# A reordered head: where four tiles of a layer norm get their scale, and which engine empties their transposes

## The chip, the cores and the metric

The kernel runs on one core of a Trainium2 chip. The metric is the device time of one execution in microseconds (us). The engines of the core are named as the profile names them: PE is TensorE, PEld its weight loads, DVE is VectorE, ACT is ScalarE, POOL is GpSimd, and SP is SyncE, which here only issues DMAs. Each engine works through its own queue in order; engines wait for each other through semaphores.

## The reference

One input x of 2048 rows by 512 columns is layer-normalized, and two branches read the normalized rows: a diagonal state-space model (branch A) and a gated feed-forward network (branch B). The output is the sum of x and both branches.

```python
xn = _layernorm(x, axis=-1)                      # (x - mean) / sqrt(var + 1e-5)
# A: complex state of 512, h[t] = Lam_bar * h[t-1] + B_bar xn[t]
#    y[t] = 2 Re(C h[t]) + xn[t] * Dskip
# B: (silu(xn @ w_gate) * (xn @ w_up)) @ w_down,  w_gate and w_up 512 x 1376
return x + A(xn) + B(xn)
```

Input and output are bf16.

## The kernel before

The 2048 rows are 16 tiles of 128 rows (`NT`), four tiles to a chunk (`TPC`), four chunks (`NCH`). TensorE needs the normalized rows transposed, with the 512 columns on the partitions, in `xnT`: four column blocks (`KD`), of which the first two and the last two are here called the first and the second contraction half (`HK` is two). Everything behind the head runs chunk by chunk: gate and up projections (`gu_mm`, L421), input projections of the state-space model (`bproj_tile`, L346), rotations and scans on VectorE (L356 to L388), and two output products (L501, L510). VectorE's work there is put into a list with a cost for each item, and `pump` issues items as TensorE's work is issued. The kernel is written under a manual schedule: each engine does its instructions in the order of the program text.

The head, L596 to L650, takes the first chunk's four tiles one by one, while their loads come in, so that TensorE can start before the chunk is complete. For a tile n it needs:

- statistics (`bn_stats`, `bn_aggr` on VectorE) that give mean and variance in `mv`;
- `rstd`, the reciprocal root. There are two ways: `rstd_act` (L177) takes a logarithm and an exponential on ScalarE, both within the table set loaded at L596; `ln_rstd` (L182) adds epsilon on VectorE and takes a power on POOL (L184);
- `norm_dve` (L190), the normalization on VectorE, here in place in `xall`;
- `xT_pe` (L202): four transposes by TensorE, two into each of two PSUM tiles, and for each PSUM tile a copy into `xnT`, by ScalarE (L218) or VectorE (L216). With `prm_too` a small transpose of twelve parameter rows (L239) is written behind the second pair.

Then `head_mm(which, lo, hi, ks, fis)` (L588) issues, for the gate (`which` 0) or the up weights (1), the matmuls of tiles lo to hi, over the column blocks `ks`, for the weight column blocks `fis`. The results of the first three weight blocks (`H`) accumulate in six PSUM banks that are held until all four tiles are through. `dummy(n, cols)` issues n matmuls on ones into one of these banks, before it is used.

The order of the text before: all rstd but tile 0's come from POOL. ScalarE copies the transposes of tiles 0, 1 and 2, VectorE those of tile 3. Tile 1 is normalized in two halves of 256 columns; tile 2's statistics are taken in two halves around them (L606, L609). TensorE takes tile 0's gate matmuls first, both contraction halves, and puts tile 1's transposes between its up matmuls. Tile 3's transposes stand in the midst of tile 2's up matmuls. An `iota` for a later table is issued on POOL at L623.

After the head's matmuls `params_a`, `params_a2` and `params_sin` compute small parameters (with a table load on ScalarE at L248), and L650 on is the steady part. The first matmul behind the head is the first of line L421. The transposes of later chunks are made by DMA (L223).

Of the kernel before, what the change touches and what calls it, by code (L numbers as in the profile page):

```python
# [10 lines left out]
F32 = mybir.dt.float32  # L11
# [12 lines left out]
def kernel(  # L24
# [17 lines left out]
    nc = tc.nc  # L42
    _, L, D = A_x.shape
# [3 lines left out]
    CW = 512  # L47
# [4 lines left out]
    KD = D // 128  # L52
# [11 lines left out]
    const = ctx.enter_context(tc.tile_pool(name="const", bufs=1))  # L64
# [8 lines left out]
    def bank(shape=(128, CW), dtype=F32):  # L73
        return psum.tile(list(shape), dtype, name="ps")
# [10 lines left out]
    xall = const.tile([128, NT, D], BF16, name="xall")  # L85
# [4 lines left out]
    for gi, (a, b) in enumerate(fgroups):  # L90
        cols = min(F, b * 128) - a * 128
# [12 lines left out]
    def wslice(groups, fi, k):  # L104
        for (a, b), t in zip(fgroups, groups):
            if a <= fi < b:
                return t[:, k, (fi - a) * 128:(fi - a) * 128 + fsz[fi]]
# [48 lines left out]
    ident = const.tile([128, 128], BF16, name="ident")  # L156
    make_identity(nc, ident[:])
    jidx = const.tile([128, CW], F32, name="jidx")


    stats = const.tile([128, NT, 6], F32, name="stats")
    stats2 = const.tile([128, 2, 6], F32, name="stats2")
    mv = const.tile([128, NT, 2], F32, name="mv")
    ve = const.tile([128, NT], F32, name="ve")
    rstd = const.tile([128, NT], F32, name="rstd")
# [4 lines left out]
    def xn_tile(c):  # L170
        return xn_end if c == NCH - 1 else xall[:, c * TPC:(c + 1) * TPC, :]

    def ln_stats(n):
        nc.vector.bn_stats(out=stats[:, n, :], in_=xall[:, n, :])  # L174
        nc.vector.bn_aggr(out=mv[:, n, :], in_=stats[:, n, :])  # L175

    def rstd_act(n):  # L177

        nc.scalar.activation(out=ve[:, n:n + 1], in_=mv[:, n, 1:2], func=ACT.Ln, bias=eps_t[:, 0:1])
        nc.scalar.activation(out=rstd[:, n:n + 1], in_=ve[:, n:n + 1], func=ACT.Exp, scale=-0.5)  # L180

    def ln_rstd(a, b):  # L182
        nc.vector.tensor_scalar(out=ve[:, a:b], in0=mv[:, a:b, 1], scalar1=EPS, scalar2=None, op0=ALU.add)  # L183
        nc.gpsimd.tensor_tensor(out=rstd[:, a:b], in0=ve[:, a:b], in1=neg_half[:, 0:b - a], op=ALU.pow)  # L184
# [2 lines left out]
        nc.vector.scalar_tensor_tensor(out=nb[:, a:b], in0=mv[:, a:b, 0], scalar=-1.0, in1=rstd[:, a:b],  # L187
                                       op0=ALU.mult, op1=ALU.mult)

    def norm_dve(n, cols=slice(0, D)):  # L190
        c, i = divmod(n, TPC)
        nc.vector.tensor_scalar(out=xn_tile(c)[:, i, cols], in0=xall[:, n, cols], scalar1=mv[:, n, 0:1],  # L192
                                scalar2=rstd[:, n:n + 1], op0=ALU.subtract, op1=ALU.mult)

    def norm_act(n):
# [3 lines left out]

    HK = KD // 2  # L200

    def xT_pe(n, halves=(0, 1), on_dve=False, prm_too=False):  # L202

        c, i = divmod(n, TPC)
        for h in halves:
            tp = bank((128, HK * 128 + 3 * NQ), BF16)
            for k in range(HK):
                lo = (h * HK + k) * 128
                nc.tensor.transpose(out=tp[:, k * 128:(k + 1) * 128], in_=xn_tile(c)[:, i, lo:lo + 128],  # L209
                                    identity=ident[:])  # L210
            if prm_too and h == 1:
                prm_transpose(tp[:, HK * 128:])
            dst = xnT[:, h * HK:(h + 1) * HK, n * 128:(n + 1) * 128]
            src = tp[:, 0:HK * 128].rearrange("p (k t) -> p k t", k=HK)
            if on_dve:
                nc.vector.tensor_copy(out=dst, in_=src)  # L216
            else:
                nc.scalar.copy(out=dst, in_=src)  # L218
        return tp[:, HK * 128:]
# [18 lines left out]
    def prm_transpose(pp):  # L238
        nc.tensor.transpose(out=pp, in_=prm_rows[:], identity=ident[0:3 * NQ, 0:3 * NQ])  # L239
# [5 lines left out]
    def params_a2():  # L245
        V.tensor_tensor(out=dre[:], in0=dt_t[:], in1=lre, op=ALU.mult)
        nc.scalar.activation(out=r_t[:], in_=dre[:], func=ACT.Exp)
        nc.scalar.preload_act_table_set("silu_and_others")  # L248
        V.scalar_tensor_tensor(out=ws2[:, 0, :], in0=dt_t[:], scalar=INV_2PI, in1=lim, op0=ALU.mult, op1=ALU.mult)
# [37 lines left out]
    def params_sin():  # L287

        def turns(dst, shift):
            src = ws2[:]  # L290
            if shift:
                V.tensor_scalar(out=dst[:], in0=src, scalar1=shift, scalar2=None, op0=ALU.add)
                src = dst[:]
            V.tensor_scalar(out=kk[:], in0=src, scalar1=MAGIC, scalar2=MAGIC, op0=ALU.add, op1=ALU.subtract)
            tt(dst[:], src, kk[:], ALU.subtract)

        V.tensor_scalar(out=ws2[:, 1, :], in0=ws2[:, 0, :], scalar1=float(CW), scalar2=None, op0=ALU.mult)
        turns(fs1, 0.0)
        nc.scalar.activation(out=sin1[:], in_=fs1[:], func=ACT.Sin, scale=TWO_PI_LO)
        turns(fc1, 0.25)  # L300
        nc.scalar.activation(out=cos1[:], in_=fc1[:], func=ACT.Sin, scale=TWO_PI_LO)
# [261 lines left out]
    H = 3  # L563
# [3 lines left out]
    def dummy(n, cols):  # L567
        for _ in range(n):
            nc.tensor.matmul(warm[:, 0:cols], lhsT=ones[:, 0:128], rhs=ones[:, 0:cols], start=True, stop=True)  # L569

    def ln_rest(c, on_act):
        ops = [(0.7, lambda n=n: ln_stats(n)) for n in range(c * TPC, (c + 1) * TPC)]
        def fin():
            ln_rstd(c * TPC, (c + 1) * TPC)
        def nbf():
            ln_nb(c * TPC, (c + 1) * TPC)
        ops += [(0.1, fin)]
        tail = [(0.1, nbf)] if on_act else []
        for n in range(c * TPC, (c + 1) * TPC):
            def one(n=n):  # L580
                (norm_act if on_act else norm_dve)(n)
                xT_dma(n)
            tail.append((0.05 if on_act else 0.35, one))
        return ops, tail
# [3 lines left out]
    def head_mm(which, lo, hi, ks, fis):  # L588

        for fi in fis:  # L590
            for k in ks:
                nc.tensor.matmul(held[fi][which][:, lo * 128:hi * 128], lhsT=wslice((wg_g, wu_g)[which], fi, k),  # L592
                                 rhs=xnT[:, k, lo * 128:hi * 128], start=(k == 0), stop=(k == KD - 1))

    allk = range(KD)
# [3 lines left out]
    rstd_act(0)  # L599
    nc.vector.bn_stats(out=stats[:, 1, :], in_=xall[:, 1, :])  # L600
    norm_dve(0)
    nc.vector.bn_aggr(out=mv[:, 1, :], in_=stats[:, 1, :])
    ln_rstd(1, 2)
    xT_pe(0)
    dummy(6, 128)
    nc.vector.bn_stats(out=stats2[:, 0, :], in_=xall[:, 2, 0:D // 2])  # L606
    norm_dve(1, slice(0, D // 2))
    norm_dve(1, slice(D // 2, D))
    nc.vector.bn_stats(out=stats2[:, 1, :], in_=xall[:, 2, D // 2:D])  # L609
    nc.vector.bn_aggr(out=mv[:, 2, :], in_=stats2[:].rearrange("p h s -> p (h s)"))  # L610
    ln_rstd(2, 3)

    head_mm(0, 0, 1, range(0, HK), (0, 1))
    head_mm(0, 0, 1, range(HK, KD), (0, 1))
    xT_pe(1, (0,))
    head_mm(1, 0, 1, allk, (0,))
    xT_pe(1, (1,))
    head_mm(1, 0, 1, allk, (1,))
    nc.vector.bn_stats(out=stats[:, 3, :], in_=xall[:, 3, :])
    norm_dve(2)  # L620
    nc.vector.bn_aggr(out=mv[:, 3, :], in_=stats[:, 3, :])
    ln_rstd(3, 4)
    nc.gpsimd.iota(out=jidx[:], pattern=[[1, CW]], base=0, channel_multiplier=0,  # L623
                   allow_small_or_imprecise_dtypes=True)
    head_mm(0, 1, 2, range(0, HK), (0, 1))
    head_mm(0, 1, 2, range(HK, KD), (0, 1))
    head_mm(1, 1, 2, allk, (0, 1))
    head_mm(0, 0, 2, allk, (2,))
    pp = xT_pe(2, prm_too=True)
    head_mm(1, 0, 2, allk, (2,))  # L630
    norm_dve(3)
    params_a(pp)
    params_a2()
    head_mm(0, 2, 3, range(0, HK), range(H))
    head_mm(0, 2, 3, range(HK, KD), range(H))
    head_mm(1, 2, 3, allk, (0,))
    xT_pe(3, on_dve=True)
    head_mm(1, 2, 3, allk, (1, 2))
    params_sin()
    tables = table_ops()  # L640
    stats1, norm1 = ln_rest(1, False)
# [60 lines left out]
    stats2, norm2 = ln_rest(2, True)  # L702
# [68 lines left out]
```

## Time and profile before

| | |
|---|---|
| time, median of 3 runs | 180.82 us (180.65 to 181.29) |
| profiled execution, its time | 180.69 us |
| its span in the profile | 178.9 us |
| PE busy | 173.6 us (97%) |
| DVE busy | 153.4 us (86%) |
| ACT busy | 93.8 us (52%) |
| POOL busy | 24.9 us (14%) |
| DMA | 15.53 MB, mean 87 GB/s |
| first transpose of tile 0 (L209) starts | 5.64 us |
| first matmul of L421 starts | 12.99 us |

The span is what the profile sees, from the first to the last instruction; the time of the execution has 1.79 us more around it. A row of the timeline gives the start, the time from the first start to the last end, the engine, the line, the operation, what is written and read, and the count; in brackets stands the idle time of the engine in front of it and what ended it. Matmuls are pipelined: one row's duration is longer than the distance between two starts.

### The profile page before, as it was taken

How to read it: one execution, taken by the hardware profiler on the slowest of the kernel's cores; microseconds unless marked ns; L12 is line 12 of the kernel's file. 1: busy time of each engine (PE TensorE's matmuls, PEld its weight loads, DVE VectorE, ACT ScalarE, POOL GpSimd, SP SyncE). 2: the span in 40 equal slices, each digit the busy share in tenths (PEclk: the TensorE clock that was granted, in tenths of full speed). 3: DMA queues.
4: the chain of work that ended last, by engine and by line, in shares of the span. 5: the costliest groups of instructions: out<-in, count | busy, mean ns of one | idle time of the engine just before them, and what ended most of it. 6: DMA issues, size and time to landing. Idle time of an engine off the chain costs nothing.

```text
span 178.9 us, 2451 instructions
## 1 busy us (share of the span) xinstructions
PE 173.6 (97%) x904; PEld 83.5 (47%) x920; DVE 153.4 (86%) x234; ACT 93.8 (52%) x170; POOL 24.9 (14%) x32
## 2 busy tenths in 40 slices
PE   8899999999999999999999999999999999999993
PEld 3684444443444444444444444444444444444743
DVE  1879997999999999999999999999999999950033
ACT  2469876988399957022998661014866610230000
POOL 5223000000500000027200000013405000150000
DMA  6999557994138400021930000007295900073012
GB/s 158 316 288 217 104 107 198 346 182 93 26 64 234 179 0 0 0 20 15 132 72 2 0 0 4 0 0 67 33 135 73 166 2 0 0 79 38 4 47 70
DMA packets 29515, 15.53 MB, mean 87 GB/s; under 512 B 18336, under 2 KB 29440, under 8 KB 29472
## 3 DMA queue, kind: packets, MB, share of 16 engines
q1 hardware_dynamic: 24416, 11.21, 26.4%
q0 software_dynamic: 3456, 3.28, 14.4%
q10 hardware_dynamic: 1632, 0.89, 1.7%
q8 instruction: 7, 0.11, 0.3%
q14 instruction: 4, 0.03, 0.1%
HBM read 8.03 MB, written 5.24 MB: 74 GB/s over the span
## 4 chain that ended last, share of the span: by engine, by line
PE 95%; DMA 2%; DVE 1%; issue 1%
PE ps L421 36%; PE ps L501 21%; PE ps L346 15%; PE ps L510 15%; PE ps L592 3%; PE ps L447 2%; DMA xall<-in_A_x_dram 2%; PE ps L457 1%; PE ps L209 1%; DVE stats L174 0%; DVE stats L600 0%; DVE xall L192 0%; PE ps L569 0%; DVE res L513 0%; DVE mv L175 0%
## 5 line engine op out<-in xcount | busy, mean ns | idle before, releaser
L501 PE MATMUL ps<-wd_sb,guT 128*128 128x512 bf16 (+4 forms) x195 | 38.6, 355 | 0.2
L421 PE MATMUL ps<-xnT,wg 128*128 128x512 bf16 x143 | 37.6, 379 | 0.3
L421 PE MATMUL ps<-xnT,wu 128*128 128x512 bf16 x146 | 37.6, 379 | 0.1
L388 DVE TENSOR_TENSOR_SCAN g<-r_t,car,u 128x512 bf16<-128x512 f32 x24 | 28.9, 1262 | 0.0
L510 PE MATMUL ps<-CF,wt 128*128 128x512 bf16 (+2 forms) x140 | 28.1, 355 | 0.2
L346 PE MATMUL ps<-xnT,BT 128*128 128x512 bf16 x126 | 28.2, 379 | 0.1
L501 PEld LDWEIGHTS <-guT 128*128 128x128 bf16 (+1 forms) x198 | 18.5, 98 | 19.9
L516 ACT CAST res<-ps 128x512 bf16<-128x512 f32 x12 | 7.0, 585 | 38.3 <-PE ps L510 38.3
L435 ACT ACTIVATE guT<-ps 128x512 bf16<-128x512 f32 x40 | 24.8, 619 | 3.6 <-PE ps L421 3.4
L436 ACT CAST u<-ps 128x512 bf16<-128x512 f32 x40 | 24.2, 606 | 4.0 <-PE ps L421 4.0
L517 POOL DMA_DIRECT2D out_dram<-res x12 | 11.1, 999 | 86.9 <-ACT res L516 86.9
L421 PEld LDWEIGHTS <-wu 128*128 128x128 bf16 x148 | 14.5, 98 | 17.5
L421 PEld LDWEIGHTS <-wg 128*128 128x128 bf16 x148 | 14.3, 98 | 17.6 <-issue 0.8
L510 PEld LDWEIGHTS <-wt 128*128 128x128 bf16 x144 | 13.4, 98 | 14.3
L346 PEld LDWEIGHTS <-BT 128*128 128x128 bf16 x128 | 12.5, 98 | 15.1
L348 ACT CAST u<-ps 128x512 bf16<-128x512 f32 x32 | 17.5, 590 | 2.9 <-PE ps L346 2.8
L513 DVE TENSOR_TENSOR res<-ps,xn_end 128x512 bf16<-128x512 f32 (+2 forms) x6 | 3.0, 514 | 14.4 <-PE ps L510 14.4
L440 DVE TENSOR_TENSOR guT<-guT,u 128x1024 bf16<-128x1024 bf16 x20 | 13.5, 680 | 0.0
L184 POOL TENSOR_TENSOR rstd<-ve,neg_half 128x1 f32<-128x1 f32 (+1 forms) x6 | 6.9, 1155 | 40.2 <-DVE ve L183 40.2
L174 DVE BATCH_NORM_STATS2 stats<-xall 128x6 f32<-128x512 bf16 x13 | 8.7, 669 | 2.8 <-DMA xall<-in_A_x_dram 2.8
L356 DVE TENSOR_TENSOR pm<-u,c 128x2048 bf16<-128x2048 bf16 x8 | 9.8, 1220 | 1.2 <-ACT c L273 1.1
L356 DVE TENSOR_TENSOR pm<-g,c 128x2048 bf16<-128x2048 bf16 x8 | 9.7, 1217 | 0.1
(105 smaller groups left out, 158.2 us busy)
## 6 DMA issues: line engine op xcount, KB each, us to landing
out_dram<-in_A_x_dram SPq DMA_DIRECT2D x1, 1536.0 KB, 7.9
out_dram<-res POOLq DMA_DIRECT2D x12, 128.0 KB, 3.1
out_dram<-xall POOLq DMA_DIRECT2D x3, 512.0 KB, 5.9
wd_sb<-in_B_w_down_dram SPq DMA_DIRECT2D x1, 1280.0 KB, 10.1
xall<-in_A_x_dram SPq DMA_DIRECT2D x1, 1024.0 KB, 6.4
wg<-in_B_w_gate_dram SPq DMA_DIRECT2D x2, 384.0 KB, 5.4
wu<-in_B_w_up_dram SPq DMA_DIRECT2D x2, 384.0 KB, 5.6
wu<-in_B_w_up_dram ACTq DMA_DIRECT2D x2, 256.0 KB, 5.2
```

Source lines behind the costliest of these rows:

```text
L174: nc.vector.bn_stats(out=stats[:, n, :], in_=xall[:, n, :])
L346: nc.tensor.matmul(ps[:], lhsT=BT[:, part, k, q * 128:(q + 1) * 128], rhs=xnT[:, k, c * CW:(c + 1) * CW], start=(k == 0), stop=(k == KD - 1))
L348: nc.scalar.copy(out=u_tiles[c][:, part, q, :], in_=ps[:])
L356: V.tensor_tensor(out=t[:], in0=flat(src()[:, i]), in1=flat(tab[:]), op=ALU.mult)
L388: V.tensor_tensor_scan(out=g()[:, part, q, :], data0=r_t[:, q:q + 1].to_broadcast([128, CW]), data1=u_tiles[c][:, part, q, :], initial=ini ...
L421: nc.tensor.matmul(ps[:fs, lo:hi], lhsT=wslice(groups, fi, k), rhs=xnT[:, k, c * CW + lo:c * CW + hi], start=(k == 0), stop=(k == KD - 1))
L435: nc.scalar.activation(out=guT[:fs, fi, :], in_=psg[:fs], func=ACT.Silu)
L436: nc.scalar.copy(out=u_pair[c][:fs, fi % 2, :], in_=psu[:fs])
L440: products.append(lambda: V.tensor_tensor(out=g, in0=g, in1=u, op=ALU.mult))
L501: nc.tensor.matmul(o[:], lhsT=gu_tiles[c][:fsz[fi], fi, i * 128:(i + 1) * 128], rhs=wd_sb[:fsz[fi], fi, lo:hi], start=(fi == 0), stop=False)
L510: nc.tensor.matmul(o[:], lhsT=w_tiles[c][:, part, q, i * 128:(i + 1) * 128], rhs=CF[:, part, q, lo:hi], start=False, stop=(part == 1 and q ...
L517: nc.gpsimd.dma_start(out=out_v[:, n, lo:hi], in_=res[:, lo:hi], accum_op=ALU.add)
```

## The change

All edits lie in the head and in the two helpers that it calls. rstd of tiles 1, 2 and 3 comes from ScalarE like tile 0's. Their places in ScalarE's queue are: tile 1's before the copy of tile 0, tile 2's behind the copies of tile 1, and tile 3's behind tile 2's. `xT_pe` takes the set of halves that VectorE copies: the first half of tile 0, and both halves of tiles 2 and 3; tile 1 and the second half of tile 0 stay with ScalarE. Tile 1 is normalized whole and tile 2's statistics are taken whole; the tile `stats2` goes. For tiles 0, 1 and 2 TensorE now takes the first contraction half for gate and up and then the second half for both; the transposes of the next tile (1) or of tile 3 stand between the halves. There are four small dummies in place of six, and the iota is issued on POOL right behind the identity.

```diff
@@ constants
     jidx = const.tile([128, CW], F32, name="jidx")
+    nc.gpsimd.iota(out=jidx[:], pattern=[[1, CW]], base=0, channel_multiplier=0, allow_small_or_imprecise_dtypes=True)
-    stats2 = const.tile([128, 2, 6], F32, name="stats2")
@@ helpers
-    def norm_dve(n, cols=slice(0, D)):
+    def norm_dve(n):
...
-    def xT_pe(n, halves=(0, 1), on_dve=False, prm_too=False):
+    def xT_pe(n, on_dve=(), prm_too=False):
...
-        for h in halves:
+        for h in range(2):
...
-            if on_dve:
+            if h in on_dve:
@@ head
-    ln_rstd(1, 2)
-    xT_pe(0)
-    dummy(6, 128)
-    nc.vector.bn_stats(out=stats2[:, 0, :], in_=xall[:, 2, 0:D // 2])
-    norm_dve(1, slice(0, D // 2))
-    norm_dve(1, slice(D // 2, D))
-    nc.vector.bn_stats(out=stats2[:, 1, :], in_=xall[:, 2, D // 2:D])
-    nc.vector.bn_aggr(out=mv[:, 2, :], in_=stats2[:].rearrange("p h s -> p (h s)"))
-    ln_rstd(2, 3)
+    rstd_act(1)
+    xT_pe(0, on_dve=(0,))
+    dummy(4, 128)
+    norm_dve(1)
+    ln_stats(2)
 
     head_mm(0, 0, 1, range(0, HK), (0, 1))
+    head_mm(1, 0, 1, range(0, HK), (0, 1))
+    xT_pe(1)
+    rstd_act(2)
     head_mm(0, 0, 1, range(HK, KD), (0, 1))
-    xT_pe(1, (0,))
-    head_mm(1, 0, 1, allk, (0,))
-    xT_pe(1, (1,))
-    head_mm(1, 0, 1, allk, (1,))
+    head_mm(1, 0, 1, range(HK, KD), (0, 1))
     nc.vector.bn_stats(out=stats[:, 3, :], in_=xall[:, 3, :])
     norm_dve(2)
     nc.vector.bn_aggr(out=mv[:, 3, :], in_=stats[:, 3, :])
-    ln_rstd(3, 4)
-    nc.gpsimd.iota(out=jidx[:], pattern=[[1, CW]], base=0, channel_multiplier=0,
-                   allow_small_or_imprecise_dtypes=True)
+    rstd_act(3)
     head_mm(0, 1, 2, range(0, HK), (0, 1))
+    head_mm(1, 1, 2, range(0, HK), (0, 1))
     head_mm(0, 1, 2, range(HK, KD), (0, 1))
-    head_mm(1, 1, 2, allk, (0, 1))
+    head_mm(1, 1, 2, range(HK, KD), (0, 1))
     head_mm(0, 0, 2, allk, (2,))
-    pp = xT_pe(2, prm_too=True)
+    pp = xT_pe(2, on_dve=(0, 1), prm_too=True)
     head_mm(1, 0, 2, allk, (2,))
     norm_dve(3)
     params_a(pp)
     params_a2()
     head_mm(0, 2, 3, range(0, HK), range(H))
+    head_mm(1, 2, 3, range(0, HK), range(H))
+    xT_pe(3, on_dve=(0, 1))
     head_mm(0, 2, 3, range(HK, KD), range(H))
-    head_mm(1, 2, 3, allk, (0,))
-    xT_pe(3, on_dve=True)
-    head_mm(1, 2, 3, allk, (1, 2))
+    head_mm(1, 2, 3, range(HK, KD), range(H))
```

## The prediction

> **What bounds the kernel now.** I read the page's busy shares and slices first, then the chain that ended last in order of time, then the timeline of the first 14 us engine by engine. The page and the chain:
>
> ```profile
> PE 173.6 (97%) x904; PEld 83.5 (47%) x920; DVE 153.4 (86%) x234; ACT 93.8 (52%) x170; POOL 24.9 (14%) x32
> ...
> PE 95%; DMA 2%; DVE 1%; issue 1%
> ...
> 7.58 1.73 PE ps L592 x24
> 9.31 0.22 PE ps L209 x4
> ...
> 13.43 6.64 PE ps L421 x30
> 20.06 4.10 PE ps L346 x19
> ```
>
> From 12.99 us (the first L421 matmul) to 176 us the chain is TensorE alone, and its matmuls there start every 0.216 us without a hole, apart from single missing records: 30 matmuls of L421 take 6.64 us, 19 of L346 take 4.10. Nothing ahead of 12.99 is hidden by anything, and nothing behind it waits. So the change is worth what it moves the first L421 matmul, one for one, provided that nothing behind it becomes late.
>
> The head, TensorE's timeline and then the three others':
>
> ```profile
> 5.64 0.40 PE L209 MATMUL ps<-ident,xall 128*128 128x128 bf16 x4 [0.81 <-DVE xall L192]
> 5.88 0.51 PE L569 MATMUL ps<-const-bfloat16-1.0 128*128 128x128 bf16 x6
> 6.39 0.66 PE L592 MATMUL ps<-xnT,wg 128*128 128x128 bf16 x8
> 6.96 0.28 PE L209 MATMUL ps<-ident,xall 128*128 128x128 bf16 x2
> ...
> 7.71 0.72 PE L592 MATMUL ps<-xnT,wg 128*128 128x128 bf16 x8
> 8.27 0.61 PE L592 MATMUL ps<-xnT,wu 128*128 128x128 bf16 x8
> ...
> 10.02 0.83 PE L592 MATMUL ps<-xnT,wg 128*128 128x128 bf16 x12
> ```
>
> ```profile
> 4.61 0.29 ACT L179 ACTIVATE ve<-mv,eps_t 128x1 f32<-128x1 f32 x1 [0.55 <-DVE mv L175]
> 4.94 0.20 ACT L180 ACTIVATE rstd<-ve 128x1 f32<-128x1 f32 x1
> 5.97 0.65 ACT L218 COPY xnT<-ps 128x256 bf16<-128x256 bf16 x2 [0.83 <-PE ps L209]
> ```
>
> ```profile
> 5.17 0.41 DVE L192 TENSOR_SCALAR xall<-xall,mv,rstd 128x512 bf16<-128x512 bf16 x1
> ...
> 9.97 0.63 DVE L192 TENSOR_SCALAR xall<-xall,mv,rstd 128x512 bf16<-128x512 bf16 x1 [0.66 <-POOL rstd L184]
> ...
> 11.23 0.49 DVE L216 COPY xnT<-ps 128x256 bf16<-128x256 bf16 x2
> ```
>
> ```profile
> 5.95 0.58 POOL L184 TENSOR_TENSOR rstd<-ve,neg_half 128x1 f32<-128x1 f32 x1 [2.34 <-DVE ve L183]
> ...
> 9.89 0.56 POOL L623 IOTA jidx<- 128x512 f32 x1
> ```
>
> Of a matmul row 0.22 us is its own length; starts lie 0.0555 apart (x12 in 0.83: (0.83-0.22)/11). I call that a slot; a 256-wide matmul is two. From 5.64 to 12.99 are 7.35 us. In it stand 16 transposes, 6 dummies and 88 matmuls, 8 of them wide: 118 slots, 6.55 us, and 0.11 for the parameter transpose. The other 0.69 us are holes, found by adding slots to each start (0.71 by the rounded starts): 0.17 before 6.39 (tile 0's first copy), 0.13 before 6.96 (second copy 0.05, tile 1's normalization 0.08), 0.07 before 7.71 and 0.12 inside the eight that follow (tile 1's two copies), 0.15 around the parameter transpose at 9.47, 0.07 at 11.77 (tile 3's second copy). Those 0.69 and two dummies (0.11) are all that the head can give: 0.80 us.
>
> **The change part by part.** The sum is made against the profiled execution, 180.69 us (span 178.9, 1.79 around it). The median of the three runs, 180.82, stands 0.13 above it. I work out when each group starts in the changed kernel, taking 0.05 us from a producer's end to its consumer (tile 0's normalization ends at 5.58, its transposes start at 5.64) and 0.04 from a matmul's end to a copy.
>
> Up to 5.64 only the iota differs: it now follows the identity on POOL (free at 3.61) and runs to about 4.2, beside tile 0's statistics (3.67, 0.69 us, on the path). Lower bound nothing; upper bound 0.22, from the normalization at 9.97, which took 0.63 beside the same iota where others of its shape take 0.41. I take nothing, because statistics beside a POOL instruction took 0.68 (L619, next to the power at 8.01) and 0.66 alone (L600). The Trainium skill ("SBUF — State Buffer", Who interferes with whom) says that VectorE contends with GpSimd only in its two-port modes or with two SBUF inputs; the 0.63 row agrees, but no run here shows statistics beside an iota. By that rule the sum stays as it is; by the 0.63 row it loses 0.22.
>
> Tile 0's first half: VectorE starts its copy when the second transpose is out (5.97). A copy takes 0.28 (L216; two took 0.49) against 0.37 on ScalarE: 6.25, matmuls from 6.31 instead of 6.39, gain 0.08. The dummies end in a hole anyway, so two fewer bring nothing else; if the copy came earlier than 6.21, they would bring up to 0.11. The Trainium skill speaks against this placing: "VectorE: DVE Perf Modes", The TRN2 errata, gives for a PSUM source 120 cycles at 0.96 GHz plus one per element, 0.39 us unaccelerated, against 0.36 on ScalarE. By it the gain would shrink by 0.11. The trace has 0.28 against 0.37, so the trace decides.
>
> Tile 1's rstd on ScalarE: its variance is ready at 5.68; 0.04, then 0.29 + 0.03 + 0.20 as in tile 0, is 6.24, where add and power gave 6.53. These two now stand in ScalarE's queue ahead of tile 0's second copy, which starts at 6.15 to 6.24 (neighbours on this engine overlap by some 0.1) and ends by 6.61. It was done at 6.61 before too, and now eight matmuls (gate and up on the first half) and four transposes lie ahead of its user, due at 6.98. Cover: 0.3 us; without it the old 0.05 hole returns. VectorE normalizes tile 1 whole at 6.28 to 6.69 (0.41; in halves 0.60); transposes possible at 6.74, TensorE arrives at 6.75. Both holes of 0.13 go, with no slack at the second.
>
> Tile 1's copies remain on ScalarE: second transpose out at 7.03, copies end at 7.44 and 7.71. TensorE has done tile 0's second half by 7.42 and starts at 7.49: a hole of 0.07. The eight first-half matmuls cover the second copy. Holes 0.19 become 0.07: gain 0.12.
>
> Tile 2: its logarithm waits behind tile 1's copies on ScalarE, where POOL stood free before. Statistics (0.66) and aggregation end at 7.48; ScalarE is free at about 7.61, rstd at 8.14, normalization 8.17 to 8.59, ready 8.64. TensorE, after 16 slots and four wide matmuls, comes at 8.81. Slack 0.17; beyond it each delay shows in full. The second weight groups landed 5.9 and 6.0 us after their issues at 2.20 and 2.29, thus by 8.3, and are wanted from 8.38 (8.71 before).
>
> Tile 3: VectorE now has tile 2's two copies ahead of tile 3's normalization, so that waits for TensorE's transposes: copies 9.13 to 9.63, normalization 9.55 to 9.96 (no iota beside it now), ready 10.02. TensorE passes the parameter transpose (0.15 hole stays, 9.24), four wide and twelve first-half matmuls: 10.35. Slack 0.33. The copies end at 11.16, inside the twelve second-half matmuls that run to 11.24: the 0.07 hole goes. Twenty-four matmuls later L421 starts at 12.57.
>
> Behind the head: the table load (1.28) follows r_t about 0.6 earlier, the first Silu starts near 12.3 instead of 12.87, VectorE's next statistics near 12.1 instead of 12.61, their data landed by 9.8. SP's queue stands as it was. The rotated outputs of chunk 0 are written by 64.0 us and the last coefficients of CF by 70.9, and both are read from 75.4, so nothing there is tight. What the three additions and powers and the halved statistics took on VectorE and POOL is in the starts above.
>
> Sum: -0.08 -0.13 -0.12 -0.07 = -0.40 us; 180.69 - 0.40 = 180.29, and 180.42 from the median's level. That is 0.22%, inside the 0.3% (0.54 us) which a measurement of this kernel can tell from no change.
>
> **The rivals.** *More holes close.* If tile 1's copies run 0.07 sooner and the parameter transpose fits its gap, and the dummies' share comes, the floor is -0.80: 179.89. For it: only starts that are modelled to 0.05 stand between. Against: the 0.15 belongs to the parameter transpose and is untouched. Everything from -0.54 on counts here: 179.9 to 180.15.
>
> *The iota costs.* 0.22 on the path by the row above: 180.51. Against it the 0.68 row.
>
> *ScalarE paces tile 2: slower.* Place: the logarithm of tile 2, the first in this kernel to stand behind copies. It decides once ScalarE is late by 0.17, takes the whole gain at 0.57, and is slower by 0.3% at 1.11. Price: a table load there (1.28 by L248) would put the transposes of tile 2 at 10.04 instead of 8.81, +1.23 - 0.40: 181.52. Against: the exponential L243 followed copies without a load, and the changed list of instructions has only the two loads of before.
>
> *VectorE's queue paces tile 3.* With both copies at ScalarE's 0.37 (+0.18) and the normalization at 0.63 (+0.22) it is 0.40 late, 0.33 covered: 180.36. Only 1.27 would make it slower.
>
> **How the numbers follow.** Forecast (with VectorE's queue, which hardly differs) 0.50: 180.1 to 180.5, of which 0.08 is beyond 0.54. More holes 0.25. Iota 0.10, within 0.3%. ScalarE 0.06, slower. A loss that no row here shows, in the 163 us behind the head, 0.09, slower. Faster 0.33, same 0.52, slower 0.15. Range 179.8 (the floor less 0.1, as runs differ) to 181.0 (beyond it lies most of the slower cases; the runs of before reach 181.29).
>
> **What would show it.** After: first L592 row at 6.31, sixteen transposes in four unbroken fours, tile 1's at 6.75, tile 2's at 8.81, tile 3's at 10.35, first L421 at 12.57. Tile 0's transposes later than 5.64 mean the iota; later than 8.81 with an idle VectorE, ScalarE; a hole behind 12.57, a loss that I have not seen.

## The result, and the profile after

The changed kernel takes 180.22 us (median of 7 runs, 180.19 to 180.44) against 180.82 (7 runs); the ratio is 0.9969, with a 95% interval of 0.9955 to 0.9983. The forecast was 180.3, and the head was to give 0.40 us. The same kernel once more, in a longer comparison, gave 0.9974 (0.9964 to 0.9984): 180.24 against 180.72.

The page after, the shares and the chain that ended last:

```profile
PE 174.8 (98%) x918; PEld 83.4 (47%) x918; DVE 153.1 (86%) x232; ACT 93.9 (53%) x173; POOL 23.2 (13%) x29
...
PE 98%; DVE 0%; issue 0%
```

TensorE's timeline of the changed head; the first matmul of L421 now starts at 12.50 us, where it was 12.99:

```profile
5.53 0.42 PE L209 MATMUL ps<-ident,xall 128*128 128x128 bf16 x4
5.78 0.40 PE L569 MATMUL ps<-const-bfloat16-1.0 128*128 128x128 bf16 x4
6.21 0.38 PE L592 MATMUL ps<-xnT,wg 128*128 128x128 bf16 x4
6.43 0.39 PE L592 MATMUL ps<-xnT,wu 128*128 128x128 bf16 x4
6.66 0.39 PE L209 MATMUL ps<-ident,xall 128*128 128x128 bf16 x4
...
7.39 0.38 PE L592 MATMUL ps<-xnT,wg 128*128 128x128 bf16 x4
...
8.72 0.39 PE L209 MATMUL ps<-ident,xall 128*128 128x128 bf16 x4
9.04 0.18 PE L239 MATMUL ps<-ident,prm_rows 12*128 12x12 bf16 x1
...
10.26 0.39 PE L209 MATMUL ps<-ident,xall 128*128 128x128 bf16 x4
...
12.50 1.03 PE L421 MATMUL ps<-xnT,wg 128*128 128x512 bf16 x4
```

VectorE, ScalarE and POOL beside it:

```profile
3.55 0.69 DVE L174 BATCH_NORM_STATS2 stats<-xall 128x6 f32<-128x512 bf16 x1 [2.65 <-DMA xall<-in_A_x_dram]
...
5.87 0.29 DVE L216 COPY xnT<-ps 128x256 bf16<-128x256 bf16 x1 [0.31 <-PE ps L209]
6.16 0.41 DVE L192 TENSOR_SCALAR xall<-xall,mv,rstd 128x512 bf16<-128x512 bf16 x1
6.48 0.69 DVE L174 BATCH_NORM_STATS2 stats<-xall 128x6 f32<-128x512 bf16 x1
```

```profile
5.92 0.20 ACT L180 ACTIVATE rstd<-ve 128x1 f32<-128x1 f32 x1
6.03 0.35 ACT L218 COPY xnT<-ps 128x256 bf16<-128x256 bf16 x1
```

```profile
3.56 0.56 POOL L159 IOTA jidx<- 128x512 f32 x1
```

Three numbers are compared from here on: the start (first transpose of tile 0), the head (from there to the first matmul of L421) and the rest (from there to the end of the span). The rest was 165.90 to 165.94 us in every profile of this case. Whatever the change did, it did in front of that matmul. The head fell from 7.35 to 6.97, 0.38 us; the start fell from 5.64 to 5.53, where the load of tile 0 had landed 0.12 us earlier in the profile after.

### The profile page after: what moved, and what is told of

Its sections match the earlier page's. It is cut to its first block, busy times and chain, and to the rows that moved or that the text cites. A ratio compares the mean times of both kernels' runs of the same rounds, so it can differ in the third digit from the quotient of the medians.

```text
span 178.4 us, 2463 instructions
## 1 busy us (share of the span) xinstructions
PE 174.8 (98%) x918; PEld 83.4 (47%) x918; DVE 153.1 (86%) x232; ACT 93.9 (53%) x173; POOL 23.2 (13%) x29
## 3 DMA queue, kind: packets, MB, share of 16 engines
HBM read 8.03 MB, written 5.24 MB: 74 GB/s over the span
## 4 chain that ended last, share of the span: by engine, by line
PE 98%; DVE 0%; issue 0%
PE ps L421 36%; PE ps L501 21%; PE ps L510 16%; PE ps L346 15%; PE ps L592 3%; PE ps L569 3%; PE ps L447 2%; PE ps L457 1%; PE ps L209 1%; DVE res L513 0%; PE ps L239 0%
## 5 line engine op out<-in xcount | busy, mean ns | idle before, releaser
L501 PE MATMUL ps<-wd_sb,guT 128*128 128x512 bf16 (+3 forms) x198 | 38.8, 356 | 0.0
L421 PE MATMUL ps<-xnT,wg 128*128 128x512 bf16 x148 | 38.0, 380 | 0.0
L421 PE MATMUL ps<-xnT,wu 128*128 128x512 bf16 x148 | 38.0, 379 | 0.0
L421 PEld LDWEIGHTS <-wu 128*128 128x128 bf16 x148 | 14.5, 98 | 17.5
L421 PEld LDWEIGHTS <-wg 128*128 128x128 bf16 x148 | 14.3, 98 | 17.6 <-issue 0.8
L174 DVE BATCH_NORM_STATS2 stats<-xall 128x6 f32<-128x512 bf16 x14 | 9.4, 670 | 2.6 <-DMA xall<-in_A_x_dram 2.6
L184 POOL TENSOR_TENSOR rstd<-ve,neg_half 128x4 f32<-128x4 f32 x3 | 5.3, 1750 | 41.9 <-DVE ve L183 41.9
```

The source lines that it names most:

```text
L421: nc.tensor.matmul(ps[:fs, lo:hi], lhsT=wslice(groups, fi, k), rhs=xnT[:, k, c * CW + lo:c * CW + hi], start=(k == 0), stop=(k == KD - 1))
L501: nc.tensor.matmul(o[:], lhsT=gu_tiles[c][:fsz[fi], fi, i * 128:(i + 1) * 128], rhs=wd_sb[:fsz[fi], fi, lo:hi], start=(fi == 0), stop=False)
```

## Experiments

| kernel | start | first L592 after the start | head | first L421 |
|---|---|---|---|---|
| before | 5.64 | 0.75 | 7.35 | 12.99 |
| before, second profile | 5.17 | 0.75 | 7.77 | 12.94 |
| changed | 5.53 | 0.69 | 6.97 | 12.50 |
| changed, second profile | 5.42 | 0.83 | 7.12 | 12.55 |
| e_core | 5.45 | 0.67 | 7.05 | 12.50 |
| e_pool | 5.48 | 0.78 | 7.28 | 12.76 |
| e_copy0 | 5.41 | 0.91 | 7.19 | 12.60 |
| e_order | 5.42 | 0.85 | 7.43 | 12.85 |
| b_act | 5.34 | 0.91 | 7.65 | 12.99 |
| a_stats | 5.17 | 0.67 | 7.61 | 12.78 |
| e_pad | 5.24 | 0.66 | 6.78 | 12.02 |
| e_pad5 | 5.42 | 0.80 | 7.05 | 12.47 |
| e_fine | 5.34 | 0.54 | 6.84 | 12.19 |
| b_x2 | 5.54 | 1.46 | 7.94 | 13.48 |

e_pool, e_copy0, e_order, b_act and e_pad were run once each, with the profiler; for these the rows of the profile count, and the single time says little. Where a kernel has lines more or fewer, its line numbers are shifted: L593 and L600 below are the statement of L592.

### The changed kernel again (after_again)

> The changed kernel once more. Call the head's length the time from the first transpose of tile 0 (L209) to the first matmul of L421: 7.35 us before, 6.97 in the changed kernel, 0.38 less. Theory A (the gain is closed holes in the head and nothing else): the head is again 6.97 +- 0.03, the rest behind it is 165.9 as in both profiles, and the time is 0.38 us (0.2%) below before; what was measured beyond that comes from when tile 0's load lands, which differs from run to run in both kernels. Theory B (part of the gain lies outside the head's holes, in the iota placed early, in a POOL queue without powers or in the start): the ratio stays at 0.9969 or below with a narrower interval, 0.5 us or more.

180.24 us, 0.9974 (0.9964 to 0.9984), that is 0.48 us below before. The interval, 0.29 to 0.65 us, does not decide between theory A's 0.38 and theory B's 0.5. The head was 7.12, not 6.97. TensorE's timeline, to be held against the one above:

```profile
4.14 1.49 PE L569 MATMUL ps<-const-bfloat16-1.0 128*128 128x512 bf16 x3
5.42 0.63 PE L209 MATMUL ps<-ident,xall 128*128 128x128 bf16 x4
5.85 0.57 PE L569 MATMUL ps<-const-bfloat16-1.0 128*128 128x128 bf16 x4
6.26 0.39 PE L592 MATMUL ps<-xnT,wg 128*128 128x128 bf16 x4
```

Four transposes take 0.63 instead of 0.42: their starts lie 0.107 apart, half the pace of 0.0557, until 6.17. The eleven dummies of 512 columns at the start of the program also ran to 5.42 at that pace, with starts 0.427 apart where full pace has 0.217, and held the first transpose back by some 0.3, though its tile was normalized at 5.08. In the first profile of before the full pace began near 3.9. The row of granted clock on the page shows 9 throughout, so only the starts tell it. The Trainium skill ("TensorE: Matmul & The Clock Gate", Part 1) gives 107 and 56 ns for 128 columns, cold and warm, and says that the moment of the switch differs from run to run, by 0.5 us to either side. The two paces agree with these starts; the moment differed by 3.1 us between the profiles of this case, by their starts near 3.5 in e_core and near 6.6 in e_order. One profile's head can thus be 0.1 to 0.3 us longer than another's.

This did not fall evenly on the kernels. The switch came at 3.5 to 3.9 in both profiles of before, in b_act and in e_core, at 6.4 in b_x2, and at 4.8 or later in the other nine. The first five have six small dummies behind tile 0's transposes, the nine have four or two; but those dummies come later than the early switches, and no run changes their number alone. Whether the changed kernel itself has a part in the late switch, or chance, stays open.

### What of the change is needed (e_core)

```diff
 # the changed kernel, with
-    nc.gpsimd.iota(... behind the identity)
+    nc.gpsimd.iota(... behind ln_rstd(3, 4))
-    dummy(4, 128)
+    dummy(6, 128)
-    rstd_act(2), rstd_act(3)
+    ln_rstd(2, 3), ln_rstd(3, 4)
-    pp = xT_pe(2, on_dve=(0, 1), prm_too=True)
+    pp = xT_pe(2, prm_too=True)
```

> The changed kernel with four of its parts undone: the iota late again, six dummies, rstd of tiles 2 and 3 by POOL, tile 2's copies by ScalarE. Left of the change: tile 1's rstd on ScalarE, tile 0's first copy on VectorE, tile 1 whole, and the contraction halves in order. Theory A: none of the four lay on the path, so the head is 6.97 to 7.02 us and the time is within 0.1 us of the changed kernel. Theory B: without the early iota and with the powers on POOL again the time goes back by some 0.2 us toward before.

180.33 us, 0.9979 (0.9969 to 0.9988); head 7.05, first L421 at 12.50 as in the changed kernel. The interval overlaps that of the changed kernel; the medians lie 0.09 apart, and the intervals do not exclude a loss of 0.2. The profile has two small holes that the changed kernel lacks, 0.04 ahead of tile 2's transposes and 0.03 ahead of tile 3's. In the head the four parts are thus worth some 0.07 us, which the runs cannot tell from nothing.

### rstd back to POOL (e_pool), tile 0's copy back to ScalarE (e_copy0), the old order (e_order)

```diff
 # e_pool: the changed kernel, with
-    rstd_act(1), rstd_act(2), rstd_act(3)
+    ln_rstd(1, 2), ln_rstd(2, 3), ln_rstd(3, 4)
 # e_copy0: the changed kernel, with
-    xT_pe(0, on_dve=(0,))
+    xT_pe(0)
 # e_order: the changed kernel, with
     head_mm(0, 1, 2, range(0, HK), (0, 1))
-    head_mm(1, 1, 2, range(0, HK), (0, 1))
     head_mm(0, 1, 2, range(HK, KD), (0, 1))
-    head_mm(1, 1, 2, range(HK, KD), (0, 1))
+    head_mm(1, 1, 2, allk, (0, 1))
     ...
     head_mm(0, 2, 3, range(0, HK), range(H))
-    head_mm(1, 2, 3, range(0, HK), range(H))
-    xT_pe(3, on_dve=(0, 1))
     head_mm(0, 2, 3, range(HK, KD), range(H))
-    head_mm(1, 2, 3, range(HK, KD), range(H))
+    head_mm(1, 2, 3, allk, (0,))
+    xT_pe(3, on_dve=(0, 1))
+    head_mm(1, 2, 3, allk, (1, 2))
```

> The changed kernel with rstd of tiles 1, 2 and 3 by VectorE's addition and POOL's power again. Theory A: tile 1's normalization starts 0.29 us later, its transposes wait with TensorE idle for 0.27 us in front of them, tiles 2 and 3 stay hidden; head 7.24 us, that is 0.27 above the changed kernel and 0.11 below before. The rival, that the order of the matmuls alone makes the gain: head 7.0 us or less.

Head 7.28 and 180.45 us; theory A had 7.24. VectorE's timeline shows the power as the wait, and TensorE's transposes of tile 1 come at 6.87, 1.39 after the start instead of 1.13:

```profile
5.92 0.29 DVE L216 COPY xnT<-ps 128x256 bf16<-128x256 bf16 x1 [0.21 <-PE ps L209]
6.40 0.41 DVE L192 TENSOR_SCALAR xall<-xall,mv,rstd 128x512 bf16<-128x512 bf16 x1 [0.19 <-POOL rstd L184]
```

> The changed kernel with both copies of tile 0 on ScalarE again, behind tile 1's logarithm and exponential. Theory A: the first copy starts only when the exponential is out, about 0.65 us after the first transpose, the first L592 matmul starts 0.92 us after it instead of 0.69, and the head is 7.22 us: most of the gain is gone, though only one copy was moved. The rival, that the matmuls' order hides it: head 7.0 us.

Head 7.19 and 180.30 us; theory A had 7.22. The copy starts only behind the exponential, and the first matmul says for whom it waited:

```profile
5.80 0.20 ACT L180 ACTIVATE rstd<-ve 128x1 f32<-128x1 f32 x1
5.91 0.63 ACT L218 COPY xnT<-ps 128x256 bf16<-128x256 bf16 x2
```

```profile
6.31 0.38 PE L592 MATMUL ps<-xnT,wg 128*128 128x128 bf16 x4 [0.28 <-ACT xnT L218]
```

> The changed kernel with the matmuls of tiles 0, 1 and 2 in the old order (gate with both contraction halves, then up; tile 3's transposes in the midst of tile 2's up matmuls); rstd, copies and normalization stay as changed. Theory A: the holes of 0.05 in front of tile 0's second half, 0.05 in front of tile 1's second half and 0.07 in front of tile 3's second half come back; head 7.11 us, 0.14 above the changed kernel (6.97). The rival, that rstd and copies alone make the gain: 7.0 us.

Head 7.43 and 180.52 us; theory A had 7.11. TensorE stayed at half pace until about 6.6 in this profile, which lengthens the head by some 0.33 (0.17 until the first L592 matmul, 0.16 in the four that follow) and covers the first of the three expected holes. The other two are there, 0.05 in the eight gate matmuls of tile 1 and 0.07 ahead of tile 3's second half:

```profile
7.62 0.66 PE L592 MATMUL ps<-xnT,wg 128*128 128x128 bf16 x8
8.12 0.61 PE L592 MATMUL ps<-xnT,wu 128*128 128x128 bf16 x8
...
11.44 0.46 PE L592 MATMUL ps<-xnT,wg 128*128 128x128 bf16 x4
11.73 0.39 PE L592 MATMUL ps<-xnT,wu 128*128 128x128 bf16 x4
```

Eight matmuls take 0.50 from start to start where eight slots are 0.45, and four take 0.29 instead of 0.22. With the 0.33 these two holes make up the 0.46 above the changed kernel; the first hole is not shown.

### One part alone (b_act)

```diff
 # the kernel before, with
-    ln_rstd(1, 2)
+    rstd_act(1)
-    ln_rstd(2, 3)
     ...
     xT_pe(1, (1,))
+    rstd_act(2)
     ...
-    ln_rstd(3, 4)
+    rstd_act(3)
```

> The kernel before with one part of the change alone: rstd of tiles 1, 2 and 3 by ScalarE, at the changed places; the copies, the halves and the order stay as before. Theory A: tile 1's exponential stands ahead of tile 0's first copy on ScalarE and delays it by 0.2 us, more than the earlier rstd gives back; the head is 7.44 us against 7.35 before, so the part alone loses 0.1. The rival, that each part brings its share by itself: the 0.27 that undoing it costs the changed kernel would show as a head of 7.08 us.

First L421 at 12.99 and 180.68 us beside a median of 180.71: nothing gained. The first matmul came 0.91 after the start, as in e_copy0, and it names the copy:

```profile
6.25 0.66 PE L592 MATMUL ps<-xnT,wg 128*128 128x128 bf16 x8 [0.16 <-ACT xnT L218]
6.96 0.28 PE L209 MATMUL ps<-ident,xall 128*128 128x128 bf16 x2
```

The head of 7.65 is 0.21 above the forecast of 7.44. That is a hole ahead of tile 1's transposes at 6.96, which the theory had closed. VectorE stood idle for 0.85 here until tile 2's load landed at 6.21; the next run shows what hangs on it. With no power left ahead of it on POOL, the iota ran at 3.56 in this kernel too, so its edit moved that as well.

### The kernel before again (before_again), and tile 2's statistics put back (a_stats)

> The kernel before, once more, as its own control. Theory A: the head is 7.35 us when the clock is up in time, and 165.92 us lie behind it; the start (first transpose of tile 0) lies anywhere between 5.4 and 5.7, with the landing of tile 0's load, and when the matmuls of the start still run at half pace the head is longer by 0.05 us for each that does. The rival, that the changed kernels start earlier for a reason of their own: this start is again 5.6 or later, while the five profiles with the change or parts of it have 5.41 to 5.53.

180.75 against 180.71, ratio 1.0006 (0.9996 to 1.0015): no change is read as no change. The rival is wrong, for this profile of before started at 5.17, the earliest but for one tie. Theory A missed as well: the full pace began near 3.5, and yet the head was 7.77, not 7.35, and the first L421 came at 12.94, only 0.05 earlier than with the start at 5.64. TensorE's and VectorE's timelines:

```profile
5.17 0.40 PE L209 MATMUL ps<-ident,xall 128*128 128x128 bf16 x4 [0.47 <-DVE xall L192]
...
5.92 0.66 PE L592 MATMUL ps<-xnT,wg 128*128 128x128 bf16 x8
6.91 0.28 PE L209 MATMUL ps<-ident,xall 128*128 128x128 bf16 x2 [0.33 <-DVE xall L192]
```

```profile
5.24 0.15 DVE L183 TENSOR_SCALAR ve<-mv 128x1 f32<-128x1 f32 x1
6.18 0.43 DVE L606 BATCH_NORM_STATS2 stats<-xall 128x6 f32<-128x256 bf16 x1 [0.79 <-DMA xall<-in_A_x_dram]
6.52 0.58 DVE L192 TENSOR_SCALAR xall<-xall,mv,rstd 128x256 bf16<-128x256 bf16 x2
```

In the kernel before, the first half of tile 2's statistics (L606) stands on VectorE ahead of tile 1's normalization, and it waits 0.79 us for tile 2's load, which landed at 6.15 (issued at 1.66, 4.5 on the way). Tile 1 could have been normalized from about 6.05 (L183 ends at 5.39, the power follows 0.08 later and takes 0.58). An early landing of tile 0 therefore gave nothing. In the first profile of before tile 0 landed late (start 5.64) and tile 2 early (5.95), so that POOL's power at 6.53 came after these statistics at 6.40, and the dependence did not show. The change removed it too, by putting all of tile 2's statistics behind tile 1's normalization.

```diff
 # a_stats: the changed kernel, with
+    nc.vector.bn_stats(out=stats2[:, 0, :], in_=xall[:, 2, 0:D // 2])
     norm_dve(1)
-    ln_stats(2)
+    nc.vector.bn_stats(out=stats2[:, 1, :], in_=xall[:, 2, D // 2:D])
+    nc.vector.bn_aggr(out=mv[:, 2, :], in_=stats2[:].rearrange("p h s -> p (h s)"))
```

> The changed kernel with one thing put back: the first half of tile 2's statistics stands ahead of tile 1's normalization on VectorE. Theory C (formed on the second profile of before: there these statistics waited for tile 2's load, landed at 6.15, and held tile 1's transposes until 6.91 although TensorE was free from 6.42): tile 1's transposes start 0.78 us after tile 2's load lands, or 0.27 later than in the changed kernel, whichever is later; the first L421 matmul comes at 12.8 to 13.0 whenever the head starts, and an early start gives nothing. In time 0.2 to 0.4 us of the gain goes. Theory A without C (the load of tile 2 is in time anyway): only the 0.27 for the 0.43 of statistics ahead, the same for every start.

180.50 us, ratio 0.9989 (0.9978 to 1.0000), 0.26 above the changed kernel's repetition. Tile 2 landed at 6.11, and tile 1's transposes started 0.82 behind it, at 6.93; the first L421 came at 12.78 although the start was 5.17:

```profile
6.13 0.43 DVE L607 BATCH_NORM_STATS2 stats<-xall 128x6 f32<-128x256 bf16 x1 [0.35 <-DMA xall<-in_A_x_dram]
6.48 0.40 DVE L193 TENSOR_SCALAR xall<-xall,mv,rstd 128x512 bf16<-128x512 bf16 x1
```

```profile
6.06 0.39 PE L593 MATMUL ps<-xnT,wu 128*128 128x128 bf16 x4
6.93 0.40 PE L210 MATMUL ps<-ident,xall 128*128 128x128 bf16 x4 [0.49 <-DVE xall L193]
```

Theory C holds: the wait for the load stands in VectorE's row, and with theory A alone the early start would have given an L421 at some 12.4 (5.17 and a head of 7.24). By the medians this one instruction costs more than half of the gain; the time alone, 0.26, would fit either theory.

### From the other side (b_x2)

```diff
 # the kernel before, with
+    nc.sync.dma_start(out=xall[:, 2, :], in_=x_v[:, 2, :])
     load_w1(nc.sync, wg_g, wg_v, 0)
     load_w1(nc.scalar, wu_g, wu_v, 0)
-    nc.sync.dma_start(out=xall[:, 2, :], in_=x_v[:, 2, :])
```

> The kernel before with tile 2's load issued ahead of the first gate weights on SP's queue, nothing else. Theory C from the other side: tile 2's load now lands near 5 us instead of 5.9 to 6.2, the half statistics ahead of tile 1's normalization never wait for it, and the head keeps its 7.35 us for every start: with the first transposes at 5.2 the first L421 matmul comes at 12.55 where the kernel before had 12.94, and the time falls by 0.1 to 0.4 us, unless the gate weights, now 0.5 us later, become the wait (then a hole in front of the first L592 matmul shows it). Theory A without C: L421 at 12.95 again, no gain.

181.19 us, ratio 1.0021 (1.0007 to 1.0036): slower by 0.2%. Tile 2's load landed at 4.90 and its statistics no longer waited, but the gate weights, issued 0.48 later, landed at 6.95 instead of 5.29, and the first matmul waited for them:

```profile
7.00 0.62 PE L592 MATMUL ps<-xnT,wg 128*128 128x128 bf16 x8 [0.34 <-DMA wg<-in_B_w_gate_dram]
```

The expectation named this way out; as a test of theory C the run decides nothing.

### Further than the change (e_pad, e_pad5, e_fine)

```diff
 # e_pad and e_pad5: the changed kernel, with
-    prm_rows = const.tile([3 * NQ, 128], BF16, name="prm_rows")
+    prm_rows = const.tile([128, 128], BF16, name="prm_rows")
+    nc.vector.memset(prm_rows[:], 0.0)
-        nc.tensor.transpose(out=pp, in_=prm_rows[:], identity=ident[0:3 * NQ, 0:3 * NQ])
+        nc.tensor.transpose(out=pp, in_=prm_rows[:], identity=ident[:])
```

> The changed kernel with the twelve parameter rows padded by zeros to 128, so that their transpose has the shape of the others. In all profiles TensorE starts the transpose of twelve rows 0.10 us late and the matmul after it 0.05 late, although nothing is waited for. If that hole belongs to the odd shape, it and half of the 0.11 go: head 6.77 us, 0.20 below the changed kernel. If it belongs to the place (the copy's PSUM tile, or the engine's wait), only some 0.05 goes: 6.92 us.

> The changed kernel with the parameter rows padded to 128, again, now timed. Its one profile had a head of 6.78 us without a hole at the parameter transpose. Expected: 0.20 us below the changed kernel, 180.0 us, and a ratio to before of 0.996; from the one time of 179.71 it could be 0.994.

Head 6.78, first L421 at 12.02 and 179.71 us in the single run: the hole belongs to the shape. Around the padded transpose TensorE has none; from tile 2's first transpose to the matmul after the parameters it takes 0.28 instead of 0.43. That is 0.15 of the 0.19 by which the head is shorter; another 0.03 is the pace, which was full here before the first transpose and not quite in the changed kernel's profile:

```profile
8.40 0.39 PE L210 MATMUL ps<-ident,xall 128*128 128x128 bf16 x4
8.62 0.22 PE L240 MATMUL ps<-ident,prm_rows 128*128 128x128 bf16 x1
8.68 0.60 PE L593 MATMUL ps<-xnT,wu 128*128 128x256 bf16 x4
```

Timed, it is 180.05 us, ratio 0.9958 (0.9943 to 0.9973), a point estimate 0.2 us below the changed kernel's, with overlapping intervals. The profile of that comparison had half pace until 6.1 and the second group of up weights landing 6.8 us after its issue at 2.29, with TensorE idle for 0.11 until then; its head was 7.05.

```diff
 # e_fine: the padded kernel, with
+    head_mmk(lo, hi, ks): for each block k of ks, gate then up, weight blocks 0 and 1
-    xT_pe(0, on_dve=(0,)); dummy(4, 128)
+    xT_pe(0, on_dve=(0,), fine=True); dummy(2, 128)      # first half: a PSUM tile and a copy for each block
-    head_mm(0, 0, 1, range(0, HK), (0, 1))
-    head_mm(1, 0, 1, range(0, HK), (0, 1))
-    xT_pe(1)
+    head_mmk(0, 1, (0, 1, 2))
+    xT_pe(1, fine=True)
     rstd_act(2)
-    head_mm(0, 0, 1, range(HK, KD), (0, 1))
-    head_mm(1, 0, 1, range(HK, KD), (0, 1))
+    head_mmk(0, 1, (3,))
     ...
+    head_mmk(1, 2, allk)                                  # tile 1, in place of its four head_mm
```

> The padded kernel, and the two copies that still leave holes cut finer: the first half of tile 0 is copied in two blocks of 128 columns by VectorE, that of tile 1 in two blocks by ScalarE, each from a PSUM tile of its own; the matmuls of tiles 0 and 1 go block by block over gate and up, and tile 1's transposes stand in front of tile 0's last block; two dummies. If a block's copy takes 0.16 us on VectorE and 0.27 on ScalarE (0.29 and 0.37 less 128 columns), the first L592 matmul starts 0.48 us after the first transpose instead of 0.69, tile 1's matmuls 1.71 instead of 1.86, and the head is 6.62 us, 0.16 below the padded kernel and 0.35 below the changed one. The rival: tile 1's normalization, which depends on none of this, is due 1.10 after the first transpose and holds everything behind it; head 6.75 us.

180.08 us, 0.9959 (0.9945 to 0.9974), the same as the padded kernel. The head was 6.84, neither 6.62 nor 6.75. A block's copy on VectorE took 0.22 instead of 0.16; then the first up weights, landed at 6.05 in this profile, ended the next hole, of 0.10:

```profile
5.88 0.27 PE L600 MATMUL ps<-xnT,wg 128*128 128x128 bf16 x2
6.09 0.28 PE L600 MATMUL ps<-xnT,wu 128*128 128x128 bf16 x2
```

The up matmuls could have followed at 5.99. In this profile the first weights' landing was thus the next bound, and the finer copies ran into it. Over the padded kernel they gained nothing that the runs can tell.

## Why the prediction was right

**What bounds.** That all behind the first L421 matmul is shifted one for one held to 0.04 us over fourteen profiles.

**Before 5.64.** The iota was priced at nothing, with 0.22 as the upper bound. Tile 0's statistics took 0.69 beside it, as they had without it. The row of statistics beside a power was the right one, and so was the Trainium skill's rule ("SBUF — State Buffer", Who interferes with whom), which no trace of this case had shown for statistics beside an iota. What the sum did not have is the pace: in the changed kernel's second profile the half pace cost some 0.3 in the start and 0.15 in the head.

**Tile 0.** VectorE's copy took 0.29 against 0.28 taken from L216, not the 0.39 that would follow unaccelerated from the formula of the Trainium skill ("VectorE: DVE Perf Modes", The TRN2 errata). That formula divides the elements by an acceleration of 2 or 4; with 2 it gives an estimate of 0.26, and the prediction gave no reason for taking it as 1. The first matmul came 0.69 after the start against 0.67 forecast: 0.06 gained instead of 0.08. In e_core and a_stats, where the full pace had begun before the start, it was 0.67.

**Tile 1.** Both holes of 0.13 went, the copy's hole stayed at 0.06 of the 0.07 expected. The wait for tile 1's rstd was read as a matter of POOL's power alone. This is the step that was incomplete: the same normalization waited behind tile 2's statistics as well, and which of the two came last depended on two landings. The sum of 0.40 is right for the profile that it was made on (0.38 measured in the head). The measured ratios say 0.56 and 0.47. That this dependence makes up the difference is argued and not shown: the two pairs of profiles give 0.49 (0.11 of it from the start) and 0.39 at the first L421 matmul, and the changed order without half pace was seen on an early start only in the padded kernel (start 5.24, head 6.78, against 5.17 and 7.77 in before). I had looked at what the removed statistics cost, and not at what they waited for.

**Tiles 2 and 3.** Tile 2's transposes came 3.19 after the start (forecast 3.17) with 0.17 of slack, tile 3's 4.74 (4.71) with 0.34; tile 3's copy hole of 0.07 went. These agree to 0.03.

**The number.** That 180.29 lies only 0.07 from the measured 180.22 is in part luck. The sum was counted from the profiled execution of before, which stood 0.13 below the median then known; from that median it gives 180.42, 0.20 too high. The mechanism was right, and the gain in time was larger than the holes that were priced.

**The rivals.** More holes did not close by themselves: that of the parameter transpose stayed, and e_pad shows that its shape made it. ScalarE kept one table set to L248, and neither its queue nor VectorE's became late. No loss showed behind the head, where the rest stayed at 165.9.

**The parts.** The forecast added them up. They don't add: the power on POOL again delays tile 1's transposes by 0.26, one copy on ScalarE lengthens the head by 0.22, while the new rstd without that copy's move gains nothing.

## What to carry to other kernels

Where one engine is full to the end, find the instruction from which it is full and count its empty time slots ahead of that: it bounds the gain before any edit is priced. When an instruction is moved ahead of another on an in-order queue, write down what it waits for, a load too, because one profile in which that load was early hides it. Look at a second profile before a sum of tenths of a microsecond is believed.

## What I had not expected of the hardware

A transpose of 12 rows between ones of 128 started 0.10 us late, and the next matmul 0.05, with nothing waited for; padded to 128 rows with zeros both holes vanished. TensorE's change to full pace came anywhere between 3.5 and 6.6 us in these profiles, unseen in the page's clock row. And the loads that the head waits for landed up to 1.0 us apart between profiles of the same order of DMAs: tile 2's at 5.75 in e_pool and at 6.75 in the changed kernel's second profile, the second up group 6.0 us behind its issue in one and 6.8 in another.
